# Convolution matmuls placed behind the feed forward's latest matmul, later requests for x and the saved sums in the last stage, and a longer pause ahead of it

## Chip, core and metric

One core of a Trainium2 chip runs the kernel. The metric is the device time of one execution in microseconds (us), as the median of several runs. Everything below on the kernel before comes from three timed runs, one profiled execution and its trace.

## What is computed

Two branches read the normalized rows of `q` and are added to `q`: a gated long convolution over time (`A`) and a feed forward with a ReLU (`B`).

```python
xn = layernorm(A_q)                                   # 2048 x 576
# A: k_shift = 4-tap causal convolution of k;  kv = k_shift * v
#    y = causal convolution of kv with ssm_k (length 2048) + kv * ssm_D
#    A = xn * y
# B: relu(xn @ w1) @ w2                               # 576 -> 4608 -> 576
out = A_q + A + B
```

The convolution is done as a Fourier transform that is written as matmuls, so both branches use TensorE (PE). All matmuls take fp32 values split into a high and a low part.

## The kernel before

**Two streams in one program.** The feed forward is the main loop: 36 weight blocks (`n`), each visited for two blocks of rows (`s`). A visit makes the hidden values (`mm1` at L569 in the first half, `quad` with `run_seq` at L545 in the second half) and queues units of the second matmul (`unit`, L632, twelve or twenty-four matmuls of 288 columns into a PSUM tile `pso`). The convolution is a generator, `conv`, that is called one step at a time from `tick`, which the feed forward calls as it emits matmuls. `tick` counts the feed forward's columns as a clock; each convolution step gives back a cost, and `rate` spreads the sum of the costs over the feed forward. A negative value stops the convolution for so many columns: that is a pause, and `PAUSES` holds their sum in units of `PAUSE` (16000 columns), so that `rate` allows for them.

**The convolution's stages.** `fk` transforms the convolution's weights (L685, tiles `ks`, `wk`), `fx` forms k_shift * v and transforms it (L685, tiles `xs`, `wx`), `fm` does the second half of the transform, the product and the first half of the way back (L904), and `fo` (from L979) does the last transform, gates it and adds it to the output. `fo` handles 16 row tiles `i`, in two units each (`n` = 0 to 31). A unit reads one tile `zo` of 128 x 1152 values from DRAM (L991, four places, requested three units ahead), and runs two times two matmuls (L1045 and L1046, `h` = 0 and 1) into PSUM tiles `psf` (three places). ScalarE (ACT) and VectorE (DVE) bring each result to `y` (L1047, L1048). One step later `gate` (L1012) multiplies `y` with the normalized x, and `add` (L1020) brings in the feed forward's sum: for the first eight tiles it adds into `acc` in SBUF, for the last eight it adds the sum `ft` that was saved to DRAM (`fin`) and stores the row tile from the POOL queue.

**Requests of the last stage.** `load_rest(i)` (L993 to L1005) requests the inverse matrix `wi` on the POOL queue, and x (`xt`, three places, two halves, L160) and the saved sum (`ft`, two places, L1004) on the SP queue. It is called for tile i+2 in step `u` = 0, `h` = 1 of tile i, just after `gate(i-1)`. The place of `xt` for tile i+2 is free once `gate(i-1)` has run, but the place of `ft` for tile i+2 is free only once `add(i)` has run, which is emitted some steps later, in tile i+1. The weight loads of the feed forward (`r`, L443 to L452) go through the same SP queue, and each of them waits for POOL's work on the block before.

**What orders the instructions.** Each engine runs its instructions in one fixed order. That order is made when the program is built, by a scheduler with a simulated timeline: an instruction may be placed ahead of others that were emitted earlier, if the simulation has its inputs ready. `tc.issue_after(x)` holds an instruction behind `x` in that order. The helper `here()` uses it for the convolution's work on ACT and DVE, which stands behind the feed forward's latest (`done["acc"]`, `done["act"]`). The convolution's matmuls have no such tie before the change. SP's DMA requests are placed by the same scheduler, and a request that waits holds up all that stand behind it in the queue.

Of the kernel before, what the change touches and what calls it, by code (L numbers as in the profile page):

```python
# [17 lines left out]
P = 128  # L18
S = 2048
D = 576  # L20
# [37 lines left out]
KT_GAP = 2000  # L58
PAUSES = 4 * NH // Q // KB * KT_GAP / PAUSE + 14
FFT_TOTAL = N_FK * W_FK + N_FX * W_FX + N_FM * W_FM + N_FO * W_FO  # L60
# [49 lines left out]
def h3_ffn_kernel(ctx: ExitStack, tc, x, k, v, shift_k, ssm_k, ssm_D, w1, w2, fwd, inv, mid, out):  # L110
# [432 lines left out]
    def run_seq(ps, seq, start=False):  # L543
        for i, (a, m) in enumerate(seq):
            nc.tensor.matmul(ps, a, m, start=start and i == 0, stop=i == len(seq) - 1,  # L545
                             skip_group_check=not start)

# [12 lines left out]
    def mm1(n, s, j):  # L560
        g = weights[n][j]
        ps = bank(j, f"psh{n}_{s}_{j}")
        seq = []
        for c in range(4):
            b = ops[s, "b2" if c % 2 else "b1"][:, :, c // 2]
            seq += [(g[:, 0, c], b[:, 0]), (g[:, 0, c], b[:, 1]), (g[:, 1, c], b[:, 0])]
        seq += rest(n, j, s)
        for i, (a, m) in enumerate(seq):
            nc.tensor.matmul(ps, a, m, start=i == 0, stop=i == len(seq) - 1)  # L569
            if i % 7 == 6:  # L570
                tick(W_PLAIN / 4)
        relu(n, s, j, ps)
# [42 lines left out]
    def unit(ns, s, b, i, h, last):  # L615
# [15 lines left out]
        for c, (a, m) in enumerate(seq):  # L631
            nc.tensor.matmul(ps[:, :NH], a, m, start=c == 0, stop=c == len(seq) - 1)  # L632
            if c % 6 == 5:
                tick(6 * NH)
# [46 lines left out]
    def first(w, stk, z, u):  # L681

        ps = fft_psum()
        for n in range(2):
            nc.tensor.matmul(ps[:, :NH], w[:, n, :], stk, start=n == 0, stop=n == 1)  # L685
        nc.scalar.activation(z, ps[:, :NH], AF.Copy)
# [8 lines left out]
    def conv():  # L695
# [179 lines left out]
        with tc.tile_pool(name="fm", bufs=2) as fp:  # L875
# [22 lines left out]
            def run(hi, lo, d, h):  # L898
# [3 lines left out]
                seq = [(m_sb[:, d, 0, :], hi), (m_sb[:, d, 0, :], lo), (m_sb[:, d, 1, :], hi)]  # L902
                for n, (a, m) in enumerate(seq):
                    nc.tensor.matmul(ps[:, :NH], a, m[:, cols], start=n == 0, stop=n == 2)  # L904
                return ps[:, :NH], cols
# [73 lines left out]
        with tc.tile_pool(name="fo", bufs=2) as fp:  # L979
            parts, rest, ys = {}, {}, {}  # L980

# [12 lines left out]
            def load_rest(i):  # L994
                if i < T:
# [4 lines left out]
                    move(xt, x, t)  # L1000
                    ft = None
                    if t < HT:
                        ft = fp.tile([P, D], F32, tag="ft", name=f"ft{t}", bufs=2)
                        nc.sync.dma_start(ft, fin[t // 2, :, t % 2, :])  # L1004
                    rest[i] = w, xt, ft  # L1005

# [8 lines left out]
            def add(i):  # L1015
                if i >= 0:
                    t = order[i]
                    to, more = (ys[i], rest[i][2]) if t < HT else (acc[t], acc[t])
                    with here():
# [9 lines left out]
            for i in range(2):  # L1029
                load_rest(i)  # L1030
            yield -2 * PAUSE
            for n, (t, u) in enumerate(units):
# [7 lines left out]
                for h in range(2):  # L1040
# [3 lines left out]
                    cols = slice(h * NH, (h + 1) * NH)  # L1044
                    nc.tensor.matmul(ps[:, :NH], w[:, u, :], hi[:, cols], start=True, stop=False)  # L1045
                    nc.tensor.matmul(ps[:, :NH], w[:, u, :], lo[:, cols], start=False, stop=True)  # L1046
# [194 lines left out]
```

## Time and profile before

| | |
|---|---|
| median of three runs | 1076.01 us (1074.57 to 1077.52) |
| profiled execution | 1079.17 us, span 1077.4 us |
| matmuls | 7153, PE busy 98% of the span |
| DVE, ACT, POOL busy | 69%, 51%, 37% |
| mean granted TensorE clock | 0.994 |
| mean DMA rate | 190 GB/s |
| last stage, first `zo` request to last store's issue | 884.28 to 1059.1 us |

The span runs from the first to the last instruction of the trace; the profiled execution's own time is 1.8 us longer. PE is busy nearly all the time, but a matmul's span in the trace overlaps the next one's, so the share says nothing of how tightly matmuls are packed. That is read from idle time, from the waits that end it, and from the granted clock.

### The profile page before, as it was taken

What the parts mean: (1) busy time and instruction counts of PE and PEld (TensorE: products, weight loads), DVE (VectorE), ACT (ScalarE), POOL (GpSimd) and SP (SyncE); (2) the same over time, 40 slices, a digit from 0 to 9 for tenths busy, and PEclk for the clock granted to TensorE, in tenths of its full rate; (3) what the DMA queues carried; (4) which work ended last, traced back from release to release, by engine and by line L of the source; (5) the groups of instructions that cost most, each with busy time, mean ns of one, the idle gap of its engine ahead of it and who ended that gap; (6) DMA issues with size and microseconds to landing.
All of it is one profiled execution on the core that took longest, in us unless ns stands there. A gap on an engine that the chain in (4) does not pass through costs nothing. (4 is left out here: it accounts for less than half of the span.)

```text
span 1077.4 us, 20001 instructions
## 1 busy us (share of the span) xinstructions
PE 1054.3 (98%) x7153; PEld 992.8 (92%) x7153; DVE 742.6 (69%) x1314; ACT 549.6 (51%) x1201; POOL 396.9 (37%) x398
## 2 busy tenths in 40 slices
PE   8999999999899999999999999999999998999998
PEld 5889999998799999999999999999999998999897
DVE  4539778779686878752487778777877755665654
ACT  4226556434433444432477787778677753443330
POOL 4133333232223233334343544434343444444531
PEclk9999999999999999999999999999999999999999
DMA  8845867778756766856875565566565559766824
GB/s 205 199 95 143 221 174 212 196 220 213 207 175 173 200 157 194 249 154 199 292 226 183 175 176 178 168 190 179 168 192 143 156 167 317 235 222 198 265 67 110
DMA packets 156303, 204.45 MB, mean 190 GB/s; under 512 B 32845, under 2 KB 122703, under 8 KB 155180
## 3 DMA queue, kind: packets, MB, share of 16 engines
q1 hardware_dynamic: 143308, 189.00, 59.3%
q0 software_dynamic: 12576, 13.44, 5.6%
q8 instruction: 56, 0.92, 0.4%
q10 hardware_dynamic: 320, 0.74, 0.3%
q14 instruction: 43, 0.35, 0.1%
HBM read 133.92 MB, written 55.05 MB: 175 GB/s over the span
## 5 line engine op out<-in xcount | busy, mean ns | idle before, releaser
L632 PE MATMUL pso<-w,hh 128*128 128x288 f32 x2304 | 470.5, 295 | 1.6 <-ACT w L531 0.8
L632 PEld LDWEIGHTS pso<-w,hh 128*128 128x128 f32 x2304 | 373.7, 188 | 10.3 <-ACT w L531 1.2
L632 PE MATMUL pso<-w,ll 128*128 128x288 f32 x1152 | 328.1, 295 | 0.0
L427 POOL TENSOR_TENSOR g<-r,g 128x256 fp32r<-128x256 f32 (+2 forms) x145 | 169.4, 1174 | 385.0 <-ACT g L469 343.8
L569 PE MATMUL psh<-b,g 128*128 128x512 f32 x864 | 218.9, 397 | 0.5 <-ACT b L223 0.2
L632 PEld LDWEIGHTS pso<-w,ll 128*128 128x128 f32 x1152 | 212.9, 188 | 1.0
L569 PEld LDWEIGHTS psh<-b,g 128*128 128x128 f32 x864 | 158.1, 189 | 31.1 <-DVE b L224 0.5
L640 DVE TENSOR_TENSOR acc<-pso,acc 128x288 f32<-128x288 f32 x232 | 102.3, 450 | 73.8 <-PE pso L632 72.8
L427 POOL TENSOR_TENSOR w<-r,w 128x576 fp32r<-128x576 f32 x72 | 115.2, 1601 | 57.8 <-ACT w L531 57.6
L551 ACT ACTIVATE hh<-psh 128x512 fp32r<-128x512 f32 x72 | 42.9, 597 | 127.1 <-PE psh L569 127.0
L552 DVE SCALAR_TENSOR_TENSOR ll<-psh,hh 128x512 fp32r<-128x512 f32 x72 | 49.3, 685 | 69.2 <-ACT hh L551 68.7
L545 PE MATMUL psb<-t,g 128*128 128x256 f32 x648 | 95.8, 281 | 0.0
L469 ACT ACTIVATE g<-r 128x256 fp32r<-128x256 f32 (+2 forms) x145 | 76.2, 542 | 33.6 <-DMA r<-in_w 25.4
L545 PEld LDWEIGHTS psb<-t,g 128*128 128x128 f32 x648 | 86.2, 189 | 0.1
L498 POOL TENSOR_TENSOR r<-r 128x256 f32<-128x256 f32 x72 | 58.0, 826 | 37.4 <-DMA r<-in_w 36.1
L545 PE MATMUL psa<-b,g 128*128 128x256 f32 x432 | 63.0, 281 | 0.4 <-ACT psa L596 0.4
L545 PE MATMUL psb<-b,g 128*128 128x256 f32 x432 | 59.6, 284 | 0.0
L545 PEld LDWEIGHTS psa<-b,g 128*128 128x128 f32 x432 | 56.6, 188 | 0.6 <-ACT psa L596 0.6
L545 PEld LDWEIGHTS psb<-b,g 128*128 128x128 f32 x432 | 56.0, 192 | 0.1
L672 POOL DMA_DIRECT2D wx<-in_fwd x32 | 17.7, 555 | 96.8 <-PE psf L685 85.6
L551 ACT ACTIVATE hh<-psa 128x512 fp32r<-128x512 f32 x36 | 21.6, 599 | 58.0 <-PE psa L545 57.7
L636 DVE SCALAR_TENSOR_TENSOR acc<-pso,rstd,acc 128x288 f32<-128x288 f32 x72 | 36.4, 510 | 20.1 <-PE pso L632 19.6
(134 smaller groups left out, 1693.7 us busy)
## 6 DMA issues: line engine op xcount, KB each, us to landing
r<-in_w SPq DMA_DIRECT2D x72, 288.0 KB, 3.6
zy<-vo SPq DMA_DIRECT2D x64, 288.0 KB, 3.1
zo<-zy SPq DMA_DIRECT2D x32, 576.0 KB, 5.8
r<-in_w SPq DMA_DIRECT2D x35, 512.0 KB, 4.5
zk<-zk SPq DMA_DIRECT2D x64, 144.0 KB, 2.5
ztk<-zk SPq DMA_DIRECT2D x32, 288.0 KB, 3.2
ztx<-zx SPq DMA_DIRECT2D x32, 288.0 KB, 3.1
k<-k SPq DMA_DIRECT2D x64, 144.0 KB, 3.2
```

The lines of the kernel that those rows point to most:

```text
L427: return nc.gpsimd.tensor_tensor(dst, src, hi, OP.subtract)
L469: nc.scalar.activation(hi, src, AF.Copy)
L498: nc.gpsimd.tensor_tensor(dst, a, b, op)
L545: nc.tensor.matmul(ps, a, m, start=start and i == 0, stop=i == len(seq) - 1, skip_group_check=not start)
L551: done["act"] = nc.scalar.activation(hh, ps, AF.Relu)
L552: lows.append(nc.vector.scalar_tensor_tensor(ll, ps, 0.0, hh, op0=OP.max, op1=OP.subtract))
L569: nc.tensor.matmul(ps, a, m, start=i == 0, stop=i == len(seq) - 1)
L632: nc.tensor.matmul(ps[:, :NH], a, m, start=c == 0, stop=c == len(seq) - 1)
L636: done["acc"] = nc.vector.scalar_tensor_tensor(acc[t][:, dc], ps[:, :NH], rstd[:, t:t + 1], acc[t][:, dc], op0=OP.mult, op1=OP.add)
L640: done["acc"] = nc.vector.tensor_tensor(acc[t][:, dc], ps[:, :NH], acc[t][:, dc], OP.add)
L672: nc.gpsimd.dma_start(w, src)
```

## The change

Four edits:

1. Every matmul of the feed forward is remembered in `done["pe"]`, and the convolution's matmuls in `first`, in `run` of the `fm` stage and in the last stage are held behind the latest one.
2. In the last stage, the request for the saved sum leaves `load_rest` and becomes `load_sum(i)`, called for tile i itself in step `u` = 0, `h` = 1, when `add(i-2)` (which frees its place) has been emitted.
3. `load_rest(i+2)` (now `wi` and `xt` alone) is called one step later, in `u` = 1, `h` = 0, behind the next `zo` request.
4. The pause ahead of the last stage grows from 2 to 3.25 `PAUSE`, that is by 20000 columns, and `PAUSES` by the same, so that `rate` rises by 1.2% and all stages run a little faster on the feed forward's clock.

```diff
-PAUSES = 4 * NH // Q // KB * KT_GAP / PAUSE + 14
+PAUSES = 4 * NH // Q // KB * KT_GAP / PAUSE + 15.25
...
     # run_seq, mm1 and unit, alike:
-            nc.tensor.matmul(ps, a, m, start=i == 0, stop=i == len(seq) - 1)
+            done["pe"] = nc.tensor.matmul(ps, a, m, start=i == 0, stop=i == len(seq) - 1)
...
     # first, run and the last stage, alike:
-            nc.tensor.matmul(ps[:, :NH], w[:, n, :], stk, start=n == 0, stop=n == 1)
+        with tc.issue_after(done["pe"].ins):
+            for n in range(2):
+                nc.tensor.matmul(ps[:, :NH], w[:, n, :], stk, start=n == 0, stop=n == 1)
...
-                    ft = None
-                    if t < HT:
-                        ft = fp.tile([P, D], F32, tag="ft", name=f"ft{t}", bufs=2)
-                        nc.sync.dma_start(ft, fin[t // 2, :, t % 2, :])
-                    rest[i] = w, xt, ft
+                    rest[i] = w, xt
+
+            def load_sum(i):
+                t = order[i]
+                if t < HT:
+                    sums[i] = fp.tile([P, D], F32, tag="ft", name=f"ft{t}", bufs=2)
+                    nc.sync.dma_start(sums[i], fin[t // 2, :, t % 2, :])
...
-            yield -2 * PAUSE
+            yield -13 * PAUSE / 4
...
                     if h == 0:
                         load_z(n + 3)
+                        if u:
+                            load_rest(i + 2)
                     else:
                         (gate if u == 0 else add)(i - 1)
                         if u == 0:
-                            load_rest(i + 2)
+                            load_sum(i)
```

The built orders hold the same 7153 matmuls, in the same sequence of the convolution's own; what moves is where they stand among the feed forward's. Three places follow, with each tile's program name and number (`zo29_12755` is the tile of unit 29). In the kernel after, L1051 and L1053 are the lines of L1045 and L1046, L994 that of L991, L1010 that of L1004, L1017 and L1025 those of L1012 and L1020, and L641 that of L640.

PE before, in the last stage, where the units 27 to 29 stand:

```order
L1045 MATMUL psf_12845<-zo27_12621,wi5_12524 128x288
L1046 MATMUL psf_12845<-zo27_12621,wi5_12524 128x288
L1045 MATMUL psf_12879<-zo28_12696,wi6_12649 128x288
L1046 MATMUL psf_12879<-zo28_12696,wi6_12649 128x288
L545 MATMUL psb34_1_12493<-t_1_5444,g34_2_12416 128x256 x6
L545 MATMUL psa34_1_12494<-b2_1_5569,g34_2_12416 128x256 x6
L545 MATMUL psa34_1_12494<-xr_1_5571,g34_3_12453 128x512 x2
L1045 MATMUL psf_12916<-zo28_12696,wi6_12649 128x288
L1046 MATMUL psf_12916<-zo28_12696,wi6_12649 128x288
L1045 MATMUL psf_12936<-zo29_12755,wi6_12649 128x288
L1046 MATMUL psf_12936<-zo29_12755,wi6_12649 128x288
```

PE now, where unit 29 stands:

```order
L632 MATMUL pso34_10_0_13121<-w2_34_0_12535,hh34_0_0_12766 128x288 x2
L632 MATMUL pso34_10_0_13121<-w2_34_0_12535,ll34_0_0_12767 128x288
L632 MATMUL pso34_10_0_13121<-w2_34_0_12535,hh34_0_1_12812 128x288 x2
L632 MATMUL pso34_10_0_13121<-w2_34_0_12535,ll34_0_1_12813 128x288
L545 MATMUL psb35_0_12848<-t_0_5321,g35_2_12770 128x256 x6
L545 MATMUL psa35_0_12849<-b2_0_5710,g35_2_12770 128x256 x6
L545 MATMUL psa35_0_12849<-xr_0_5712,g35_3_12816 128x512 x2
L1051 MATMUL psf_12954<-zo29_12780,wi6_12696 128x288
L1053 MATMUL psf_12954<-zo29_12780,wi6_12696 128x288
L1051 MATMUL psf_12972<-zo29_12780,wi6_12696 128x288
L1053 MATMUL psf_12972<-zo29_12780,wi6_12696 128x288
```

Unit 29 stood right behind unit 28, in block 34 of the weights; now it stands in block 35, with 188 more matmuls of the feed forward ahead of it.

SP's queue before, from the sum of tile 11 to the `zo` of unit 30 (the bracket names the engines or queues that the request waits for):

```order
L1004 DMA ft3_12260<-fin_89 128x576 [waits DVE_49]
L160 DMA xt5_12526<-in_x 64x576 [waits DMAHW6_49,DVE_49]
L160 DMA xt5_12526<-in_x 64x576 [waits DMAHW7_49]
L1004 DMA ft4_12394<-fin_89 128x576 [waits DMAHW0_49,DVE_49]
L160 DMA xt6_12651<-in_x 64x576 [waits DMAHW1_49,DVE_49]
L160 DMA xt6_12651<-in_x 64x576 [waits DMAHW2_49]
L443 DMA r1_35_12458<-in_w1 128x4x256 [waits DMAHW3_49,Pool_49]
L445 DMA r1_35_12458<-in_w1 64x256 [waits DMAHW4_49]
L445 DMA r1_35_12458<-in_w1 64x256 [waits DMAHW5_49]
L1004 DMA ft5_12529<-fin_89 128x576 [waits DMAHW6_49,DVE_49]
L991 DMA zo29_12755<-zy_87 128x1152 [waits DMAHW7_49,PE_49]
L991 DMA zo30_12818<-zy_87 128x1152 [waits DMAHW0_49,PE_49]
```

SP's queue now, from the `zo` of unit 26 to that of unit 30:

```order
L994 DMA zo26_12567<-zy_87 128x1152 [waits DMAHW2_49,PE_49]
L994 DMA zo27_12637<-zy_87 128x1152 [waits DMAHW3_49,PE_49]
L160 DMA xt6_12698<-in_x 64x576 [waits DMAHW4_49,DVE_49]
L160 DMA xt6_12698<-in_x 64x576 [waits DMAHW5_49]
L994 DMA zo28_12694<-zy_87 128x1152 [waits DMAHW6_49,PE_49]
L1010 DMA ft5_12795<-fin_89 128x576 [waits DMAHW7_49,DVE_49]
L994 DMA zo29_12780<-zy_87 128x1152 [waits DMAHW0_49,PE_49]
L452 DMA r2_35_1_12727<-in_w2 128x2x288 [waits DMAHW1_49,Pool_49]
L160 DMA xt7_12831<-in_x 64x576 [waits DMAHW2_49,DVE_49]
L160 DMA xt7_12831<-in_x 64x576 [waits DMAHW3_49]
L1010 DMA ft6_12925<-fin_89 128x576 [waits DMAHW4_49,DVE_49]
L994 DMA zo30_12827<-zy_87 128x1152 [waits DMAHW5_49,PE_49]
```

Before, five requests of x and the sums that wait for DVE, and a weight load, stood between the `zo` of unit 28 and that of unit 29; now one or two tiles' requests stand between one `zo` and the next.

DVE before, around the last `add` of the program (`y7`, tile 15):

```order
L640 TENSOR_TENSOR acc10_6121<-pso34_10_0_13121,acc10_6121 128x288
L600 TENSOR_TENSOR psa35_1_13023<-psb35_1_13022,m5_35_1_13036 128x256
L1020 SCALAR_TENSOR_TENSOR y7_12995<-y7_12995,rstd_84,ft7_12797 128x576
L640 TENSOR_TENSOR acc10_6121<-pso34_11_0_13147,acc10_6121 128x288
L640 TENSOR_TENSOR acc8_6118<-pso34_8_1_13161,acc8_6118 128x288
```

DVE now, at the same place:

```order
L1017 SCALAR_TENSOR_TENSOR y7_13000<-xt7_12831,mv_83,y7_13000 128x576
L641 TENSOR_TENSOR acc10_6147<-pso34_11_0_13147,acc10_6147 128x288
L1025 SCALAR_TENSOR_TENSOR y7_13000<-y7_13000,rstd_84,ft7_13037 128x576
L641 TENSOR_TENSOR acc8_6144<-pso34_8_1_13161,acc8_6144 128x288
L603 TENSOR_TENSOR psb35_1_13014<-psb35_1_13014,m5_35_1_13028 128x256
```

The last `add` moved behind one more eviction of the feed forward.

More of the change, by code (lines that the diff above doesn't have):

```diff
@@ L544, in run_seq @@
         for i, (a, m) in enumerate(seq):
-            nc.tensor.matmul(ps, a, m, start=start and i == 0, stop=i == len(seq) - 1,
-                             skip_group_check=not start)
+            done["pe"] = nc.tensor.matmul(ps, a, m, start=start and i == 0,
+                                          stop=i == len(seq) - 1, skip_group_check=not start)
     def relu(n, s, j, ps):
@@ L631, in unit @@
         for c, (a, m) in enumerate(seq):
-            nc.tensor.matmul(ps[:, :NH], a, m, start=c == 0, stop=c == len(seq) - 1)
+            done["pe"] = nc.tensor.matmul(ps[:, :NH], a, m, start=c == 0,
+                                          stop=c == len(seq) - 1)
             if c % 6 == 5:
@@ L683, in first @@
         ps = fft_psum()
-        for n in range(2):
-            nc.tensor.matmul(ps[:, :NH], w[:, n, :], stk, start=n == 0, stop=n == 1)
+        with tc.issue_after(done["pe"].ins):
+            for n in range(2):
+                nc.tensor.matmul(ps[:, :NH], w[:, n, :], stk, start=n == 0, stop=n == 1)
         nc.scalar.activation(z, ps[:, :NH], AF.Copy)
@@ L902, in run @@
                 seq = [(m_sb[:, d, 0, :], hi), (m_sb[:, d, 0, :], lo), (m_sb[:, d, 1, :], hi)]
-                for n, (a, m) in enumerate(seq):
-                    nc.tensor.matmul(ps[:, :NH], a, m[:, cols], start=n == 0, stop=n == 2)
+                with tc.issue_after(done["pe"].ins):
+                    for n, (a, m) in enumerate(seq):
+                        nc.tensor.matmul(ps[:, :NH], a, m[:, cols], start=n == 0, stop=n == 2)
                 return ps[:, :NH], cols
@@ L979, in conv @@
         with tc.tile_pool(name="fo", bufs=2) as fp:
-            parts, rest, ys = {}, {}, {}
+            parts, rest, ys, sums = {}, {}, {}, {}
             order = [*range(HT, T), *range(HT)]
@@ L1017, in add @@
                     t = order[i]
-                    to, more = (ys[i], rest[i][2]) if t < HT else (acc[t], acc[t])
+                    to, more = (ys[i], sums[i]) if t < HT else (acc[t], acc[t])
                     with here():
@@ L1044, in conv @@
                     cols = slice(h * NH, (h + 1) * NH)
-                    nc.tensor.matmul(ps[:, :NH], w[:, u, :], hi[:, cols], start=True, stop=False)
-                    nc.tensor.matmul(ps[:, :NH], w[:, u, :], lo[:, cols], start=False, stop=True)
+                    with tc.issue_after(done["pe"].ins):
+                        nc.tensor.matmul(ps[:, :NH], w[:, u, :], hi[:, cols], start=True,
+                                         stop=False)
+                        nc.tensor.matmul(ps[:, :NH], w[:, u, :], lo[:, cols], start=False,
+                                         stop=True)
                     nc.scalar.activation(low[own, cols], ps[other, :NH], AF.Copy)
```

## Prediction, made before the changed kernel was run

> **What bounds the kernel now.** First the page's busy times, then PE's stretches, to see where its time isn't filled.
>
> ```profile
> PE 1054.3 (98%) x7153; PEld 992.8 (92%) x7153; DVE 742.6 (69%) x1314; ACT 549.6 (51%) x1201; POOL 396.9 (37%) x398
> ```
>
> PE is the bound, and 1077.4 - 1054.3 = 23 us is all that filling its gaps could bring, apart from the clock. The change takes no matmul away. The table of stretches says where the gaps are (columns: length, busy time of PE, PEld, DVE, ACT, POOL, granted clock, DMA share, GB/s):
>
> ```profile
> 0.00:50.00 50.00, 45.94 (x251) 35.93 (x252) 25.95 (x71) 17.99 (x35) 15.12 (x20) 1.00 0.88 209
> 200.00:300.00 100.00, 95.10 (x563) 85.99 (x562) 76.54 (x126) 39.62 (x80) 29.92 (x31) 0.98 0.78 215
> 500.00:550.00 50.00, 48.58 (x355) 46.66 (x354) 25.85 (x46) 24.91 (x54) 19.43 (x18) 1.00 0.83 263
> 550.00:884.00 334.00, 333.90 (x2554) 329.90 (x2553) 254.68 (x447) 243.43 (x546) 138.70 (x117) 1.00 0.58 173
> 884.00:1060.00 176.00, 168.57 (x1259) 165.11 (x1258) 104.73 (x192) 66.38 (x152) 79.86 (x92) 0.98 0.67 209
> ```
>
> Idle: 4.1 us at the start, 4.9 in the stage `fx`, 1.4 where `fm` begins, 0.1 in the other 334 us of `fm`, and 7.4 in the last stage. So the last stage is the largest, `fx` next. PE's own waits name the causes, as total, times and longest:
>
> ```profile
> PE psf L1045 <- DMA zo<-zy: 6.3, 4, 2.4
> PE psf L685 <- DMA xs<-both: 4.9, 2, 3.1
> ```
>
> In the last stage PE stands four times before a `zo` that hasn't landed. The timeline of PE has a fifth wait at the stage's first unit, 1.1 us, and 6.3 + 1.1 = 7.4:
>
> ```profile
> 891.48 0.37 PE L1045 MATMUL psf<-zo,wi 128*128 128x288 f32 x1 [1.14 <-ACT psa L596]
> ...
> 904.76 0.37 PE L1045 MATMUL psf<-zo,wi 128*128 128x288 f32 x1 [1.95 <-DMA zo<-zy]
> ...
> 990.15 0.37 PE L1045 MATMUL psf<-zo,wi 128*128 128x288 f32 x1 [1.68 <-DMA zo<-zy]
> ...
> 1020.54 0.37 PE L1045 MATMUL psf<-zo,wi 128*128 128x288 f32 x1 [2.42 <-DMA zo<-zy]
> ```
>
> A wait costs more than its length where the clock falls behind it, as the same table shows for shorter stretches:
>
> ```profile
> 905.00:908.00 3.00, 3.00 (x16) 3.00 (x16) 0.45 (x1) 0.50 (x2) 0.83 (x2) 0.51 1.06 320
> 908.00:911.00 3.00, 3.00 (x23) 3.00 (x23) 1.18 (x3) 2.69 (x7) 1.81 (x2) 0.92 1.03 272
> 1020.50:1024.00 3.50, 3.46 (x16) 3.30 (x17) 0.83 (x2) 1.20 (x3) 0.00 (x0) 0.59 0.28 102
> 1024.00:1027.00 3.00, 3.00 (x24) 3.00 (x24) 0.69 (x1) 0.86 (x4) 0.00 (x0) 0.91 0.00 0
> ```
>
> Lost to the clock: 3.0 x 0.49 + 3.0 x 0.08 + 3.5 x 0.41 + 3.0 x 0.09 = 3.4 us. The last stage thus loses 7.4 + 3.4 = 10.8 us.
>
> Here rule and rows differ. The Trainium skill (TensorE: Matmul & The Clock Gate, What's actually happening) says that the clock halves after at least one idle window of about 3.4 us and comes back after about as long at work. No idle time here is that long, and after 1.95 and 2.42 us the clock fell to 0.51 and 0.59; the measurement decides. By the rule the waits would cost their 7.4 us alone.
>
> Why the `zo` are late is told by the chain of waits, at two of the four places:
>
> ```profile
> 980.98 0.46 DVE acc L640
> 981.44 1.26 DVE y L1020
> 982.72 0.34 SPq L1004
> 983.16 1.26 SPq L452
> 984.52 5.50 DMA zo<-zy
> ...
> 1012.56 0.13 PE psf L1046
> 1012.75 7.65 DMA zo<-zy
> ```
>
> At 984.52 the `zo` of unit 23 is queued behind a saved sum, which waits for the `add` that frees its place: a queue that stands. At 1012.75 nothing is in front: the request goes out as unit 25's last matmul frees its place, and unit 29 comes too soon after that. The scheduler had pulled the units forward and bunched them. With four places, a `zo` has from the last matmul of unit n-4 to the first of unit n. In the order before, that is 25 matmuls of 288 columns, 24 of 256 and 2 of 512 for unit 29. The chain gives their spacing:
>
> ```profile
> 892.52 2.40 PE pso L632 x18
> ...
> 895.62 0.70 PE psb L545 x6
> ...
> 1047.18 1.16 PE psa L545 x8
> ```
>
> That is 0.133 us for 288 columns, 0.117 for 256, and, as the last row holds six of 256 and two of 512, 0.23 for 512: 3.3 + 2.8 + 0.5 = 6.6 us, where the transfer took 7.65. Counted so, 5 of the 28 units from the fifth on have less than 7.65 us before (12, 13, 17, 23 and 29), and three of PE's four waits are among these.
>
> **The change part by part.** *Order of the convolution's matmuls.* In the order now, all stand behind the feed forward's latest. In the last stage 109 of 128 stood ahead of it, the median by some 90 matmuls. Now the smallest distance from unit n-4 to unit n is that of unit 9: 51 matmuls of 288, 42 of 256 and 4 of 512, 6.8 + 4.9 + 0.9 = 12.6 us; unit 29 has 90, 54 and 6, 19.7 us; the median is 16. Against that stands what a `zo` needs:
>
> ```profile
> zo<-zy SPq DMA_DIRECT2D x32, 576.0 KB, 5.8
> ```
>
> 5.8 us in the median, 7.65 in the chain's worst. 12.6 - 7.65 leaves at least 5 us for the queue ahead of it. The bunching alone should then cost nothing more.
>
> *Requests.* The sum is asked for when its place is about to be free, and x one step later. What the queue waited before for the `add` that frees a sum's place:
>
> ```profile
> SPq L1004 <- DVE y L1020: 3.5, 2, 2.8
> ```
>
> 2.8 us at the longest fits in the 5 us. So both causes should go. Left over I take 0.8 us, half a wait of 1.7 us; the bounds are 0 and, for one wait of the size at 904.76 with its clock (1.95 + 1.7), 3.7.
>
> *Pause.* 99 of the feed forward's matmuls stood between the last matmul of `fm` and the first of the last stage, now 128: 29 more, at 0.12 to 0.13 us nearly 4 us of room, more than the first unit's wait of 1.1. That wait is in the 10.8 already.
>
> *Earlier stages.* The weights' stage and the first part of `fx` are word for word in the old order, up to the fourth stack's first pair, the two waits of 4.9 us included; so these and their clock stay. Behind that the raised rate moves `fx` up to 31 and `fm` up to 72 of the feed forward's matmuls forward, some 9 us at most. The work that feeds them on ACT and DVE is tied to the feed forward's evictions and moves too. In `fm` PE idles 0.1 us in 334; I take 0. The bounds: a wait like the longest in `fx`, 3.1 us, with the clock behind it (the stretch of 4 us that follows it),
>
> ```profile
> 276.00:280.00 4.00, 4.00 (x16) 3.39 (x16) 2.55 (x4) 0.92 (x4) 0.00 (x0) 0.63 1.03 262
> ```
>
> that is 3.1 + 4.0 x 0.37 = 4.6 us more, or the 1.4 us of idle at `fm`'s beginning gone.
>
> *End.* The later stage ends nearer to the end: 219 matmuls stood behind the convolution's last, now 130 (108 of 288, 18 of 256, 4 of 512: 17.4 us). The last `add` moves behind one more eviction. Its store (from POOL's timeline) and the end (from the chain) before:
>
> ```profile
> 1058.02 1.05 POOL L160 DMA_DIRECT2D out<-y  x2 [1.44 <-DVE y L1020]
> ...
> 1064.59 7.87 PE pso L632 x59
> ```
>
> The store was issued 13 us before the last matmul; one or two us of that are spent. Cost nothing; if the `add` came over 10 us late, it would show one for one.
>
> *Sum.* -10.8 + 0.8 = -10.0 us. The profiled execution goes from 1079.2 to 1069.2. It lies 3.2 us above the median of the runs, 1076.0; the same step from the median gives **1066.0 us**. Its own bounds: -10.8 - 1.4 = -12.2 (1063.8) and -10.8 + 3.7 + 4.6 = -2.5 (1073.5).
>
> **The rivals.** *Transfers grow into the room.* At 905 to 911 the DMA share is 1.06 and 1.03, so the 16 engines are full while a `zo` is under way. If that, and not the order, sets the landing, transfers of 12.6 us and more would leave the four waits, and the time at 1076.0; with half of the loss left, 5.4 us, it is 1070.6 + 0.8 = 1071.4. For it: these rows. Against it: over the stage the share is 0.67, and spreading the units spreads their 32 transfers too. Chance 0.16.
>
> *The queue stands in more places (slower).* In SP's order now 14 `zo` stand right behind a request of x or of a sum that waits for DVE, with at most a weight load between; before, 6. If `gate` and `add` come later than the scheduler thought, each of them can hold back a `zo`. A wait costs in the mean (1.95 + 1.68 + 2.42) / 3 = 2.0 us and 3.4 / 3 = 1.1 of clock: 3.1. From four waits on the gain is used up; from five on, 15.5 - 10.8 = 4.7 us are lost: 1080.7. For it: DVE's wait behind evictions is what held the `zo` of unit 23. Against it: it needs over 5 us of standing at each, where 2.8 was the longest. Chance 0.10.
>
> *Only the idle time comes back.* If the clock falls at its own time, whatever PE's short waits, 7.4 - 0.8 = 6.6 us are gained: 1069.4. The rows of 905 and 1020.5 speak against it, the stretch around 990.15 somewhat for it, as the clock shows no fall there:
>
> ```profile
> 988.00:992.00 4.00, 2.32 (x16) 1.98 (x16) 1.87 (x4) 1.54 (x4) 0.54 (x1) 1.00 1.05 394
> ```
>
> Chance 0.08. This is what the Trainium skill's rule on the clock, quoted above, would make of the time.
>
> *The hold does nothing.* The order rules it out for the last stage.
>
> **How the numbers follow.** 0.66 for the forecast; 0.16, 0.10 and 0.08 for the rivals. A measurement of this kernel tells about 0.3%, 3.2 us, from no change, so faster means below 1072.8. Faster: 0.64 of the forecast's 0.66 (its upper bound lies past that line), the 0.08 of idle time alone, and 0.03 of the first rival, where less than half stays: 0.75. Same: 0.02 + 0.13 = 0.15. Slower: 0.10. The range is 1062.5 to 1075: the forecast's bounds, 1.3 us more below as the three runs spread by 3 us, and above so far that it takes in the first rival but for the case in which all four waits stay. The slower rival is left out.
>
> **What would show it.** Right: no wait of PE for `zo` over 0.5 us, stretches behind 884 with PE idle under 1 us and the clock at 1.00, requests of `zo` 12 us and more ahead of their first matmul, and the waits of `fx` at 248 and 272 unchanged. Wrong: PE waiting for `zo` as before, SP standing for `y` ahead of several `zo`, new idle time in `fm` between 550 and 884, or a store of `out` from POOL that ends the chain.

## The result and the profile after

The changed kernel takes **1066.2 us** in the median of four runs (1063.4 to 1066.87), against 1076.01: a ratio of 0.9907, with a 95% interval of 0.9887 to 0.9928. The forecast was 1066.0.

The profiled execution took 1066.69 us with a span of 1064.9; that is 12.5 us less span than the profiled execution before, where the medians differ by 9.8. The one before was a long run of its kernel: 1079.17 us, where 25 further runs of it had a median of 1075.19. So the pair of traces shows a larger step than a typical pair of runs. The mean granted clock tells where the excess lies: it was 0.994 in that run, 0.997 in the median of the further ones, and 0.998 in all four runs of the changed kernel. The difference of 0.003 over 1077 us is 3.2 us, by estimate nearly the whole excess.

The page's busy times, then the table of stretches of the changed kernel (columns as before: length, busy time of PE, PEld, DVE, ACT, POOL, granted clock, DMA share, GB/s):

```profile
PE 1051.3 (99%) x7153; PEld 989.8 (93%) x7153; DVE 743.0 (70%) x1314; ACT 551.3 (52%) x1201; POOL 396.2 (37%) x398
```

```profile
0.00:50.00 50.00, 46.95 (x252) 36.38 (x253) 25.95 (x71) 17.98 (x35) 15.11 (x20) 1.00 0.88 209
200.00:300.00 100.00, 95.37 (x560) 85.90 (x559) 76.54 (x126) 39.48 (x80) 30.12 (x31) 0.98 0.76 214
500.00:550.00 50.00, 50.00 (x369) 48.69 (x369) 27.23 (x51) 26.27 (x57) 18.43 (x18) 1.00 0.82 259
550.00:884.00 334.00, 333.27 (x2542) 328.16 (x2541) 253.51 (x442) 243.33 (x543) 139.79 (x120) 1.00 0.61 182
884.00:1060.00 176.00, 175.99 (x1346) 173.40 (x1344) 109.07 (x205) 67.48 (x154) 80.55 (x89) 1.00 0.66 203
```

Read the last row first. PE was idle 7.4 us there before, and now 0.01; the clock was 0.98 and is 1.00. Idle time of PE fell from 23.1 to 13.6 us, 9.5 in all: 7.4 in the last stage, 1.4 where `fm` begins (48.58 to 50.00 busy), 0.3 in `fx` and 1.0 at the start, less 0.6 that is new in the rest of `fm`. The 1.0 at the start is no work of the change, which touches nothing there. The other 3.0 of the 12.5 us lie in busy time, 1054.3 to 1051.3, with the same 7153 matmuls: that is the clock, and it agrees with the 3.4 us counted in the prediction. By the mean clocks above, a typical pair of runs would get about 1 us of it.

PE's waits, as total, times and longest; no `zo` is among them any more, and `fx` still waits for its `xs`:

```profile
PE psf L687 <- DMA xs<-both: 3.1, 2, 2.8
PE psf L687 <- ACT both L688: 1.4, 1, 1.4
PE psf L907 <- DVE vo L963: 0.4, 1, 0.4
```

The last stage's tile `zo` (the view of one tile; the last row gives the time from a request's issue to the landing as smallest, median and largest):

```profile
L994 SPq DMA_DIRECT2D zo<-zy x32: 319/326/607, 874.3 to 1026.6; - x32
...
who waited for it (us, times):
  POOL wi L1001: 20.7, 7
  ACT low L1055: 13.8, 6
...
DMA to landing us min/median/max: 3.5/4.8/10.2
```

PE isn't among those who wait for it. The first request goes out at 874.3 instead of 884.3, so the first three tiles are there when the stage begins, and the fourth lands 22 us ahead of its use. In the trace each `zo` from the fifth on is asked for 12.6 us (unit 9) to 21.1 us (unit 6) ahead of its first matmul, and each that has a landing on record has landed at least 7.7 us ahead of it. Before, the leads of units 4, 23 and 29 were 7.2, 5.6 and 7.8 us, and without the time that PE stood for them 5.2, 3.9 and 5.4. PE took up units 23 and 29 only 0.14 us after they had landed. The median transfer, 5.8 us before, takes 4.8, which fits requests that collide less.

What SP's queue waits for in the last stage:

```profile
SPq L994 <- PE psf L1053: 56.3, 19, 8.1
```

The request for `zo` waits for its place ahead of time, and PE waits for no `zo`.

The room, which the prediction counted from the last matmul of unit n-4 to the first of unit n, is the most that a `zo` can have. What comes off it is the time for which its place is already free and its request hasn't gone out; in the text it is called the request's delay. It is 0.03 us in the median of both kernels, and at most 1.6 us (unit 20) from the fifth unit on in the changed one. Before, it was 5.4 us for unit 4, 3.3 for unit 23, 1.2 for unit 29 and 0.2 for unit 12: the four units for which PE stood 1.95, 1.68, 2.42 and 0.22 us. Unit 4 had 10.5 us of room, so the count alone did not find it. Its request went out at 897.61. It first stood behind saved sums and weight loads (their rows are shown below, with the pause alone), and from 895.6 on for a landing, as SP's queue before shows:

```profile
SPq L991 <- DMA zo<-zy: 4.5, 4, 1.9
```

The longest of these, 1.9 us, is unit 4's. The order lists show that a request on SP waits for the landing of the eighth one before it (DMAHW0 to DMAHW7 come in turn). For unit 4 that was unit 3's `zo`, asked for at 888.25 and landed at 897.53, a transfer of 9.3 us. The two other units with short room, 13 and 17 (7.5 and 7.3 us), had a delay of 0.03 us and no wait.

### The profile page after: what moved, and what is told of

Same layout as the page of the kernel before. It is cut to its first block, busy times and chain, and to the rows that moved or that the text cites. A ratio compares the mean times of both kernels' runs of the same rounds, so it can differ in the third digit from the quotient of the medians.

```text
span 1064.9 us, 19977 instructions
## 1 busy us (share of the span) xinstructions
PE 1051.3 (99%) x7153; PEld 989.8 (93%) x7153; DVE 743.0 (70%) x1314; ACT 551.3 (52%) x1201; POOL 396.2 (37%) x398
## 4 chain that ended last, share of the span: by engine, by line
PE 91%; DVE 4%; ACT 3%; issue 1%; DMA 1%; SPq 0%; ACTq 0%; DVEq 0%
PE pso L632 40%; PE psh L569 21%; PE psb L545 12%; PE psf L907 6%; PE psa L545 6%; PE psf L687 3%; PE psw L1111 1%; PE psf L1051 1%; PE psf L1053 1%; DVE both L818 1%; DMA both<-in_k 0%; DVE acc L641 0%; ACT k L938 0%; DMA xs<-both 0%; DVE yl L932 0%
## 5 line engine op out<-in xcount | busy, mean ns | idle before, releaser
L427 POOL TENSOR_TENSOR g<-r,g 128x256 fp32r<-128x256 f32 (+2 forms) x145 | 166.4, 1154 | 348.1 <-ACT g L469 289.8
L641 DVE TENSOR_TENSOR acc<-pso,acc 128x288 f32<-128x288 f32 x232 | 101.9, 451 | 61.2 <-PE pso L632 59.6
L427 POOL TENSOR_TENSOR w<-r,w 128x576 fp32r<-128x576 f32 x72 | 112.8, 1567 | 63.5 <-ACT w L531 63.5
L498 POOL TENSOR_TENSOR r<-r 128x256 f32<-128x256 f32 x72 | 62.9, 892 | 40.8 <-DMA r<-in_w 39.3
L950 DVE TENSOR_TENSOR k<-psf,k 128x288 f32<-128x288 f32 x64 | 29.1, 455 | 30.0 <-ACT sw L949 29.5
```

What stands on the lines that cost most here:

```text
L427: return nc.gpsimd.tensor_tensor(dst, src, hi, OP.subtract)
L498: nc.gpsimd.tensor_tensor(dst, a, b, op)
L641: done["acc"] = nc.vector.tensor_tensor(acc[t][:, dc], ps[:, :NH], acc[t][:, dc], OP.add)
L950: nc.vector.tensor_tensor(k1[:, cols], ps, k1[:, cols], OP.mult)
```

## The experiments

Twelve kernels were run, all on one core, each against the kernel before on the same chip. "Room" is the count that the prediction made: the time from the last matmul of unit n-4 to the first of unit n, from the order. The rows of the table are explained one by one below.

| kernel | median, us | ratio to before (95%) | PE idle 884 to 1060, us | rooms under 7.65 us |
|---|---|---|---|---|
| before (profiled run) | 1076.01 | 1 | 7.4 | 12, 13, 17, 23, 29 |
| changed | 1066.2 | 0.9907 (0.9887 to 0.9928) | 0.0 | none |
| hold alone | 1070.36 | 0.9953 (0.9935 to 0.997) | 3.4 | none |
| requests alone | 1072.8 | 0.998 (0.9963 to 0.9997) | 3.3 | as before |
| pause alone | 1068.37 | 0.9927 (0.9898 to 0.9956) | 1.0 | 11, 12, 17, 28 |
| without the hold | 1069.74 | 0.9951 (0.9936 to 0.9966) | 2.3 | 11, 12, 17, 28 |
| without the later requests | 1066.76 | 0.992 (0.9896 to 0.9944) | 0.7 | none |
| without the pause | 1071.05 | 0.9938 (0.9916 to 0.996) | 3.1 | none |
| before, five places for `zo` | 1071.23 | 0.9941 (0.9923 to 0.9959) | 1.8 | none |
| changed, three places | 1067.12 | 0.9908 (0.9891 to 0.9925) | 0.0 | 14, 17, 20 |
| hold in the last stage only | 1064.9 | 0.9894 (0.9868 to 0.9921) | 0.0 | none |
| no burst in `fx` | 1067.66 | 0.9916 (0.9896 to 0.9937) | 0.0 | none |
| no burst in `fx` and `fm` | 1067.23 | 0.9913 (0.9884 to 0.9943) | - | none |
| the same, one request on POOL | 1063.95 | 0.9883 (0.9859 to 0.9906) | - | none |

For the last two the stretch isn't comparable, since PE's last matmul ends before 1060; neither of them idles more than 0.13 us from 884 to 1040.

### Each edit alone

**The hold alone.** Requests and pause are those of before.

```diff
+    with tc.issue_after(done["pe"].ins):   # first, run and the last stage
```

> The hold alone, requests and pause as before. Theory of the room (PE waits where a unit's first matmul follows the last of the unit four earlier too soon for its zo to land): the smallest room in this order is 13.0 us where before five units had under 7.65, so the waits for zo go but for the stage's first unit (1.1 us, its pause is the old one): 1066 to 1068 us. Theory of the queue (SP stands behind requests of x and sums): the sums are requested as early as before, one to three waits of about 3 us stay: 1069 to 1073 us. Theory of the pause: no change, 1076 us.

Measured: 1070.36, ratio 0.9953. That misses the 1066 to 1068 of the theory of the order and lies in the range of the rival, the queue, but not by what the rival said: the waits for `zo` are gone. Unit 4's request still has a delay of 5.0 us, and its room is now 19.7. But the last stage isn't full. Its stretch, and PE's waits (the first is at 908, the second is the stage's first unit):

```profile
884.00:1060.00 176.00, 172.59 (x1318) 169.72 (x1316) 111.23 (x201) 66.91 (x154) 81.54 (x92) 1.00 0.72 214
```

```profile
PE pso L632 <- DVE acc L641: 2.1, 1, 2.1
PE psf L1049 <- ACT psa L596: 1.0, 1, 1.0
```

The hold takes away what it was counted for, and two other waits show: the first unit's, which the pause was to cover, and a new one of 2.1 us at 908. There DVE's `add` took 5.64 us, and the eviction that PE waits for was queued behind it. The timeline of DVE in this kernel:

```profile
904.24 5.64 DVE L1023 SCALAR_TENSOR_TENSOR acc<-y,rstd,acc 128x576 f32<-128x576 f32 x1
909.81 0.45 DVE L641 TENSOR_TENSOR acc<-pso,acc 128x288 f32<-128x288 f32 x1
```

**The later requests alone.** PE's order is that of before.

```diff
-                            load_rest(i + 2)     # at u = 0, h = 1, with the sum
+                            load_sum(i)          # and load_rest(i + 2) one step later
```

> The later requests alone; PE's order is that of before, row for row. Theory of the room: the same five units have under 7.65 us, only the wait of unit 23 (1.7 us), which a sum held up, can shrink: 1074 to 1076 us. Theory of the queue: most of the 10.8 us of the last stage comes back: 1066 to 1069 us.

Measured: 1072.8, ratio 0.998, the smallest gain of the three, and in neither of the expected ranges. PE still waits for `zo`, less than before (6.3 us, 4 times):

```profile
PE psf L1048 <- DMA zo<-zy: 2.6, 3, 1.6
```

The rooms are the same as before, but unit 29, for which PE stood 2.42 us, now has a lead of 5.7 us and PE loses 0.3 there: the transfer nearly made it in that time, where it took 7.65 before. The largest wait left, 1.6, is that of unit 4, with 10.5 us of room and a delay of 5.0. So a short room doesn't say that a wait must come, and a longer one doesn't say that none can: the delay comes off it, and the transfer isn't a constant.

**The pause alone.** Requests and order rule are those of before.

```diff
+PAUSES = 4 * NH // Q // KB * KT_GAP / PAUSE + 15.25
+            yield -13 * PAUSE / 4
```

> The longer pause alone; no hold, requests where they were. Four units (11, 12, 17, 28) keep a counted room under 7.65 us. My theory: the waits at the middle stage's beginning (1.6) and the last stage's first unit (1.1) go with the pause, those for zo stay at about 3 to 5 us: 0.995 to 0.998 of before. The rival, that pause and rate alone do most of it: 0.993 or less, with under 1.5 us idle between 884 and 1060.

Measured: 1068.37, ratio 0.9927, the largest gain of the three and the number that the rival gave. My theory missed here. Two stretches, PE's one wait for `zo`, and the transfers:

```profile
500.00:550.00 50.00, 50.00 (x375) 49.01 (x374) 28.85 (x55) 26.51 (x57) 18.44 (x18) 1.00 0.85 261
884.00:1060.00 176.00, 174.96 (x1333) 172.03 (x1333) 112.57 (x204) 66.50 (x152) 77.64 (x89) 1.00 0.65 203
```

```profile
PE psf L1046 <- DMA zo<-zy: 0.4, 1, 0.4
```

```profile
DMA to landing us min/median/max: 3.7/5.0/10.1
```

The waits at `fm`'s beginning and at the first unit are gone, as expected. What was not expected is that the waits for `zo` go too, all but 0.4, though four rooms stay short. The leads tell why. Without the time that PE stood for them, the three units that waited most had 5.2, 3.9 and 5.4 us before (units 4, 23 and 29); with the pause they have 7.4, 7.6 and 6.9, and the shortest of all are 5.9 and 6.1 (units 11 and 17), which don't wait. The stage starts 10 us sooner (its first request at 874.6 instead of 884.3) and the fifth request, unit 4's, goes out at 889.96. Before, that one came in the middle of saved sums and weight loads. SP's timeline of the kernel before, and the DMA share (the last but one number) of the stretch:

```profile
891.67 1.44 SPq L1004 DMA_DIRECT2D ft<-fin  x2
893.81 0.38 SPq L443 DMA_DIRECT2D r<-in_w  x1
894.50 1.12 SPq L445 DMA_DIRECT2D r<-in_w  x2
897.61 0.33 SPq L991 DMA_DIRECT2D zo<-zy  x1
```

```profile
892.00:900.00 8.00, 8.00 (x64) 7.95 (x64) 4.60 (x10) 2.33 (x6) 1.62 (x2) 1.00 1.10 300
```

With the pause alone the same stretch has a share of 0.90, and the delay of unit 4's request is 1.3 us. It is at most that in every kernel with the longer pause (with three places, unit 3's), and 5.0 to 5.4 in those with the old one (with five places, unit 5's is 6.5). The later requests alone leave it at 5.0, and here the weight loads still stand ahead of it. So what goes with it is the earlier start, and not the place of the sums. Units 23 and 29 gain in another way: the pause moves the units among the feed forward's matmuls, and their rooms grow from 7.3 and 6.6 us to 10.2 and 9.7. The four units with less than 7.65 have delays of at most 0.5 us and no wait. The 0.4 that is left is unit 29's, in spite of a room of 9.7, with a delay of 2.9. The runs of this kernel spread from 1067.25 to 1071.26, and the profiled one is the shortest, at a mean clock of 1.00 where the longest had 0.996.

### Each edit left out

**Without the hold.**

```diff
-    with tc.issue_after(done["pe"].ins):   # all three places
```

> Requests and pause without the hold. 102 of the last stage's 128 matmuls stand ahead of the feed forward's latest, and units 11, 12, 17 and 28 have 6.6 to 7.6 us of room. Theory of the room: two to four waits for zo of 1 to 2.5 us, part with a lower clock behind them: 1070 to 1076 us. Theories of the queue and of the pause: like the whole change, 1065 to 1067 us.

Measured: 1069.74, ratio 0.9951. One wait for `zo` of the old size is back, where two to four were expected. It is unit 29's, which has 9.7 us of room and a request that is delayed by 3.1; unit 23 (10.2 and 3.2) lands 0.1 us ahead of its matmul, and the four units with short rooms don't wait:

```profile
PE psf L1048 <- DMA zo<-zy: 1.6, 1, 1.6
```

**Without the later requests.** PE's order is that of the changed kernel.

```diff
-                            load_sum(i)
+                            load_rest(i + 2)     # at u = 0, h = 1, with the sum
```

> Hold and pause, requests as before; PE's order is that of the whole change, row for row. Theory of the room: the smallest room of 12.6 us is enough to take in SP's standing for a sum (2.8 us at the longest before): 1065 to 1067 us, no wait for zo over 0.5 us. Theory of the queue: waits behind the sums from unit 16 on, 1068 to 1072 us.

Measured: 1066.76, ratio 0.992; no wait for `zo`. Once the units are spread, the later requests bring nothing that can be measured. 12 us of lead hide a queue that stands 2.8 us.

**Without the pause.**

```diff
-            yield -13 * PAUSE / 4
+            yield -2 * PAUSE
```

and `PAUSES` as before.

> Hold and later requests with the old pause. PE's order is that of the run with the hold alone; the smallest room is 13.0 us. Theory: no wait for zo from the second unit on, but the first unit's wait (1.2 us) and the 2 us where fm begins stay, as both stand in the old order: 1068.5 to 1070.5 us. Rival (the requests matter once the units are spread): 1066 to 1067 us.

Measured: 1071.05, ratio 0.9938. No wait for `zo`, but the same losses as with the hold alone:

```profile
500.00:550.00 50.00, 47.94 (x350) 46.01 (x349) 25.11 (x44) 24.35 (x53) 19.85 (x18) 1.00 0.83 262
884.00:1060.00 176.00, 172.93 (x1318) 169.97 (x1317) 110.98 (x200) 67.51 (x154) 82.24 (x92) 1.00 0.69 213
```

2.1 us at `fm`'s beginning, 0.8 at the first unit, and 2.0 at 909 behind an `add` of 5.54 us on DVE. 1068.5 to 1070.5 were expected. So the pause is worth more than the first unit's 1.1 that the prediction gave it: 3.3 us by the two ratios (0.9938 - 0.9907), 4.6 by the two profiled spans (1069.5 and 1064.9). The 2.0 at 909 is the meeting of DVE and POOL described at the end. Only the two kernels with the hold and the old pause show one of that length, and nothing in the pause was meant for it.

**Hold in the last stage only.** The convolution's first and middle stage keep their old freedom.

```diff
-        with tc.issue_after(done["pe"].ins):   # in first and in run
```

> The whole change, but the hold stands only at the last stage's matmuls; the convolution's first and middle stage keep the old order of their matmuls. My theory: the gain comes from even units in the last stage, so this is as fast as the changed kernel, 0.990 to 0.994 of before, no wait for zo and a last stage with under 1 us idle between 884 and 1060. The rival, that the hold also removes waits in the first and middle stages: 2 to 4 us slower than the changed kernel, about 0.995, with the idle time between 200 and 884.

Measured: 1064.9, ratio 0.9894. All of the gain is there; the hold in the other stages does nothing that can be measured.

```profile
884.00:1060.00 176.00, 176.00 (x1348) 173.74 (x1348) 109.30 (x205) 67.76 (x154) 81.40 (x89) 1.00 0.67 206
```

### The room, tried without the order

**Five places for `zo` in the kernel before.** None of the change is in it; the place for it comes from one buffer of `low` instead of two.

```diff
-                    z = fp.tile([P, 2, D], F32R, tag="zt", name=f"zo{n}", bufs=4)
+                    z = fp.tile([P, 2, D], F32R, tag="zt", name=f"zo{n}", bufs=5)
...
-                        load_z(n + 3)
+                        load_z(n + 4)
```

> The kernel before, unchanged but for five places for zo in place of four, requested four units ahead (and one place for low in place of two, to make space). The units stay bunched, 106 of 128 ahead of the feed forward's latest, but the room is 10.4 us at the least and 20.9 in the median. Theory of the room: most waits for zo go, while the first unit's, fm's first and fx's stay, and the sums still stand in SP's queue: 1067 to 1071 us. Rival (the bunching itself or the queue did it): 1074 to 1076 us.

Measured: 1071.23, ratio 0.9941. PE's waits in the last stage: for `zo` 0.7 instead of 6.3 us, and the first unit's, which this doesn't touch, as before:

```profile
PE psf L1045 <- ACT psa L596: 1.1, 1, 1.1
PE psf L1045 <- DMA zo<-zy: 0.7, 1, 0.7
```

PE's order wasn't held and the pause wasn't changed, so more time for each `zo` is enough by itself to take most of these waits. The 0.7 that is left is unit 5's: it has 13.7 us of room, but its request is delayed by 6.5 and its transfer takes 7.7. The time is a little above the expected 1067 to 1071, since the wait at the first unit and others stay. This also speaks against the rival that the engines' full share sets the landing: the DMA share of this stage is 0.69, no lower than the 0.67 before, and the transfers take as long as before, 5.7 us in the median and up to 10.4.

**Three places in the changed kernel.** The reverse: the whole change, with the room taken back.

```diff
-                    z = fp.tile([P, 2, D], F32R, tag="zt", name=f"zo{n}", bufs=4)
+                    z = fp.tile([P, 2, D], F32R, tag="zt", name=f"zo{n}", bufs=3)
...
-                        load_z(n + 3)
+                        load_z(n + 2)
```

> The whole change, but three places for zo in place of four, requested two units ahead. The room runs from the last matmul of unit n-3: 12.0 us in the median, 5.9 at the least, under 7.65 for units 14, 17 and 20. Theory of the room: waits for zo come back at one to three of these units, 1067.5 to 1072 us. Rival (the bunching did it, whatever the room): no wait, 1066 us.

Measured: 1067.12, ratio 0.9908, so my expectation missed: no wait came back, as its rival said, though units 14, 17 and 20 have little room.

```profile
884.00:1060.00 176.00, 176.00 (x1348) 173.70 (x1347) 109.05 (x205) 67.74 (x154) 80.59 (x89) 1.00 0.67 205
```

```profile
DMA to landing us min/median/max: 3.5/4.3/8.9
```

The leads of units 17 and 14 are 5.7 and 5.8 us, little more than units 4 and 29 had before without their waits, and both land 1.5 and 2.0 us ahead of their matmuls, since their transfers take 4.2 and 3.8 us. Their requests have no delay. The 7.65 us that the prediction measured rooms by is what one transfer took beside others; here the median is 4.3. Spreading doesn't rule out a long one: units 2 and 26 took 8.9 and 8.0 us, with leads of 24 and 16, so that nothing waited for them.

### Toward a version that beats both

What is left is `fx`, where some 7 us go to waits and clock, before as after. In the trace its first four tiles come at once, since `tick` has saved up credit: in the changed kernel the `xs` of the second to the fourth are asked for 2.5 to 4.0 us ahead of use, the later ones 8.0 to 11.7.

**No burst in `fx`.** The saved credit is dropped as the stage begins, and `PAUSES` is raised so that the stages still end in time.

```diff
-PAUSES = 4 * NH // Q // KB * KT_GAP / PAUSE + 15.25
+PAUSES = 4 * NH // Q // KB * KT_GAP / PAUSE + 19.25
...
+                clock["conv"] = min(clock["conv"], 0.0)
                 for t in range(T):
```

> The whole change, and where the loop of fx begins the convolution's saved-up credit is set to 0 at most, with PAUSES up by 4 so that rate makes up for it. The pauses ahead of fx let the credit grow, and its first four tiles came in a burst: their stacks had 4 us from request to use, the later ones 11. In this order the second to fourth tiles stand 7 to 24 us later, the last stage ends 2.7 us earlier than in the whole change. If the burst makes fx's waits (6 us with the clock), they go: 1060 to 1062 us. If late splits on ACT make them wherever the tiles stand: 1065 to 1067 us.

Measured: 1067.66, ratio 0.9916. The waits of `fx` are gone, and as much is lost where `fm` begins:

```profile
200.00:300.00 100.00, 99.78 (x597) 90.15 (x596) 75.07 (x128) 37.56 (x75) 28.93 (x28) 1.00 0.73 204
500.00:550.00 50.00, 45.25 (x336) 44.61 (x335) 22.22 (x41) 18.92 (x42) 19.02 (x20) 0.97 0.83 254
```

```profile
PE psf L908 <- ACT k L939: 4.8, 1, 4.8
```

**No burst in `fm` either.** The same line ahead of that stage's loop.

```diff
+            clock["conv"] = min(clock["conv"], 0.0)
             for g in range(NG + 2):
```

> The kernel without the burst in the first stage, and the same line once more ahead of the middle stage's loop: the saved credit is dropped there too. My theory: the 4.9 us wait at the middle stage's beginning came from that stage's burst, in which the third group of the k side was asked for 2 us before it was needed, so it goes, and the first stage's waits stay away: span 1061 to 1063, 0.985 to 0.988 of before. The rival, that the wait is set by the depth of that stage's loads and comes back later or as two: 0.990 to 0.993, no better than the changed kernel.

Measured: 1067.23, ratio 0.9913; one of its four runs, the profiled one, took 1063.39. The rival was right: a wait of 3.4 us is still there at 541. SP's timeline shows why: three requests of the second pass's x wait for their places, and the third group of `zk` is asked for behind them.

```profile
531.65 5.28 SPq L160 DMA_DIRECT2D acc<-in_x  x3
536.98 0.58 SPq L890 DMA_DIRECT2D ztk<-zk  x1
```

**That request on POOL.**

```diff
-                    nc.sync.dma_start(raw[name, g], rows(z, g))
+                    queue = nc.gpsimd if (name, g) == ("k", 2) else nc.sync
+                    queue.dma_start(raw[name, g], rows(z, g))
```

> The kernel without the bursts in two stages, with one request more moved: the third group of the k side in the middle stage is asked for by POOL instead of SP, where it stood 5 us behind three requests of the second pass's x that waited for their places. My theory: the request goes out at 531 to 532 us instead of 537, so the 3.4 us wait of PE at the middle stage's beginning goes; no other wait over 1 us is left behind the start; the span is 1058 to 1060 and the ratio to before 0.983 to 0.988, which would beat the changed kernel (0.991). The rival, that the transfer is as late from POOL, or that the wait only moves to the next group: 0.989 to 0.992 and a wait of 2 to 4 us between 530 and 560.

Measured: 1063.95 in the median of six runs (1061.72 to 1067.43), ratio 0.9883 (0.9859 to 0.9906). The request goes out at 531.99, five us sooner, and PE's wait is 2.6 us and for something else: the product on DVE waits for the two small copies `k<-k`. The first now stands behind the same three requests, the second behind weight loads that follow. SP's timeline:

```profile
532.76 7.61 SPq L160 DMA_DIRECT2D acc<-in_x  x3
540.42 0.59 SPq L943 DMA_DIRECT2D k<-k  x1
```

The ratio lies between the two expected, 0.983 to 0.988 and the rival's 0.989 to 0.992. What stands in the queue is the cause, and taking out one request that suffers leaves the next. This kernel is the fastest by its ratio, but its interval overlaps that of the changed one, and that of the hold in the last stage only. Asking for the second pass's x later, or from another queue, wasn't tried.

## Why the prediction was right, point by point

**The bound.** Right: PE was the bound, its gaps were the prize, and the last stage had the largest part of them. It lost 10.8 us and now loses nothing.

**The room.** The mechanism holds in kind: a wait comes when the room, less the delay of the request, is shorter than the transfer. With more room the waits go, by a fifth place alone all but 0.7 us, and by the hold alone wholly. The count itself was weaker than it looked. It missed unit 4, the second largest wait, whose room was 10.5 us, and flagged units 13 and 17, which didn't wait: the delay was left out of it. The prediction saw the delay of unit 23, took unit 29 for a case with nothing in front, and had no row for unit 4. In the trace unit 25's last matmul ends at 1011.51 already (the one of 1012.56 in the chain is unit 26's), and the request for unit 29 stands 1.2 us more behind weight loads and a saved sum:

```profile
1010.85 1.15 SPq L445 DMA_DIRECT2D r<-in_w  x2
1012.09 0.54 SPq L1004 DMA_DIRECT2D ft<-fin  x1
1012.75 3.29 SPq L991 DMA_DIRECT2D zo<-zy  x3
```

In the kernels with the requests alone, the pause alone, no hold and five places, the largest wait left is each time that of a unit with over 7.65 us of room, and the units under 7.65 wait little or not at all. Nor does 7.65 hold as a constant: leads of 5.2 and 5.4 us were too short before, and 5.7 and 5.8 were enough with three places. That the change has no wait left is no luck: its least lead is 12.6 us, and the longest transfer took 10.2.

**Which edit does it.** Here the working was off, though the sum wasn't. The prediction explained the last stage by order and requests, and gave the pause the first unit's wait, 1.1 us, which "is in the 10.8 already". The runs show the pause alone at -0.7%, the hold alone at -0.5%, the requests alone at -0.2%. That is -1.4% in sum, and the whole gives -0.9%: each takes some of the same waits, and what is gone can't go again. By the ratios, leaving out the pause costs 0.3%, the hold 0.4% and the requests 0.1%, each with some 0.3% of uncertainty, so the last is none that can be told. The pause and the requests together, without the hold, come out at 0.9951, no better than the pause alone at 0.9927, within the noise. In the last stage the pause cuts the delay of unit 4's request from 5.0 to 5.4 us to 1.3, and gives units 23 and 29 more room. The beginning of `fm`, ahead of the pause, can only gain by the raised rate in `PAUSES`; how much of the rest comes by the length of the pause and how much by the rate wasn't tried apart.

**Leftover in the last stage, 0.8 us.** 0.0 in the profiled run.

**Earlier stages, 0 within +4.6 and -1.4.** `fm`'s beginning came out at the lower bound, -1.4, and the rest of `fm` at +0.6. That the pause's raised rate takes the wait at the beginning away is shown by the kernels with the pause, all of which, but for the three with dropped credit, have 50.00 us of busy time from 500 to 550, while those without it, the kernel before among them, have 47.66 to 48.58. The loss in `fx` stayed about the same, as forecast: what PE's matmuls from 200 to 300 take over their usual spacing, idle time and clock together, is by estimate 7.4 us, and was 6.8. Its waits are not the same one by one: 1.8 and 3.1 us for `xs` became 0.4 and 2.8, and one of 1.4 for ACT is new.

**Clock.** The clock came back with the waits: 0.98 to 1.00 in the last stage, so the third rival (1069.4) is out for the profiled pair. By the Trainium skill's rule of 3.4 us (TensorE: Matmul & The Clock Gate, What's actually happening) the waits would have cost their idle time alone. In the trace after, too, the clock falls behind a wait that is shorter, that of 2.8 us in `fx`:

```profile
275.00:278.00 3.00, 2.03 (x8) 2.06 (x9) 1.41 (x3) 1.90 (x4) 0.43 (x1) 0.64 0.99 284
```

But a wait of such a length does not always bring a fall. The kernel with the pause alone waited 3.1 us in `fx`, with no fall in its row:

```profile
PE psf L686 <- DMA xs<-both: 4.8, 2, 3.1
200.00:300.00 100.00, 95.04 (x567) 85.84 (x567) 77.96 (x129) 39.71 (x81) 29.72 (x30) 1.00 0.77 216
```

With the hold alone, waits of 2.8 us in `fx` and 2.1 at 908 came without one too, where 1.95 brought one before. What decides is open. Each of the two falls in the prediction's rows cost 1.7 us (1.47 + 0.24 and 1.44 + 0.27). So the term of 3.4 was read rightly from its trace, and how many falls a run has is in part chance: the further runs of the kernel before, at a mean clock of 0.997, fit fewer falls than the profiled one had at 0.994.

**The end.** Right. The store of the last row tile is issued from POOL 12.6 us ahead of the end of the last matmul, and was 13.9 before.

**The slower rival.** SP does stand for `y` behind more requests, and PE doesn't notice: no request is delayed by more than 1.6 us, and the least lead is 12.6.

**The total.** -10.0 us was forecast from the profiled run before and applied to the median; the profiled pair gave -12.5 and the medians -9.8. Of the 12.5, 1.0 lies at the start, where nothing was changed, and 1.4 at `fm`'s beginning, which the prediction had as a bound. On the other side, by the mean clocks about 2 of the 3.4 us of clock were a loss of that one run. That the medians fit to 0.2 us is thus luck, in part: terms of 1 to 2 us that the working didn't have, or had too large, cancel. The 7.4 us of idle time that the last stage gained, most of the whole, are no luck.

## What to carry to other kernels

Count, from the order, the time between the release of a buffer and its next use. Subtract the time for which the request stands in its queue after the release, which the trace shows, and set what is left against what the transfer takes in a crowd: that finds the places at risk. A fifth buffer, a spread order or an earlier start each cure much the same waits, so don't expect their gains to add. When a request moves out from behind a queue that stands, look at what is next in that queue before counting the gain. And compare medians with medians: a trace is one run, here 3 us above the middle of its kernel's runs.

## What the runs showed of the hardware

A DVE operation of 128 x 576 that takes about 1.1 us in the mean (`add` into `acc`, eight times, in the changed kernel 8.6 us in all) took 5.64 us in the kernel with the hold alone and 5.54 us in the one without the pause, each time at the same place: while POOL worked through tensor operations without a gap. POOL's timeline in the kernel with the hold alone:

```profile
904.67 0.75 POOL L498 TENSOR_TENSOR r<-r 128x256 f32<-128x256 f32 x1
905.37 1.31 POOL L427 TENSOR_TENSOR g<-r,g 128x512 fp32r<-128x512 f32 x1
906.62 1.42 POOL L427 TENSOR_TENSOR w<-r,w 128x576 fp32r<-128x576 f32 x1
908.00 1.26 POOL L427 TENSOR_TENSOR g<-r,g 128x512 fp32r<-128x512 f32 x1
```

POOL's operations keep their length, and DVE's ends at 909.88, 0.6 us behind the last of them. The traces of all fourteen kernels bear the meeting out. This `add` with `acc` took 0.80 to 0.82 us in all 29 cases in which POOL ran no tensor operation meanwhile, and 0.80 to 5.64 in the other 83. The evictions into `acc`, which read one operand from PSUM, took at most 0.46 us in all 3248 cases, 1739 of them with POOL at work. The Trainium skill (SBUF — State Buffer, SBUF: two separate sides) has a rule that fits: GpSimd and a DVE operation with two inputs in SBUF share a pair of ports, which the one that starts first holds for its whole instruction, while the other is blocked. These rows agree in that the `add`, with two operands in SBUF, is stretched and the evictions are not. The rule speaks of one instruction; that DVE stood through four of POOL's in a row is not explained by it, and no run here tells why.
